# Gate and value of a fused scan and MLP kernel from 15 slice products over three features, instead of 11 over two

## The chip, the cores and the metric

The kernel runs on one core of one Trainium2 chip. The metric is the device time of one execution in microseconds (us): 826.79 us, the median of three runs (826.69 to 827.34). Engines are named as the profile names them: PE (TensorE, matmuls), PEld (its weight loads), DVE (VectorE), ACT (ScalarE), POOL (GpSimd), SP (SyncE, which issues nearly all DMAs). SBUF is the on-chip memory, PSUM the accumulators that PE writes.

## The reference, cut to what matters

Three stages follow one another: a recurrent attention, a first MLP (the largest of three matmuls, then a projection), and a second, gated MLP. All data are fp32, 3072 tokens of width 384; the second MLP has 1536 hidden columns.

```python
def _moe_ref(x, w1, w2, w3, w_out):
    h = np.maximum(np.maximum(x @ w1, x @ w2), x @ w3)
    return (h @ w_out).astype(np.float32)

def _moe2_ref(x, w_gate, w_val, w_out):
    g = x @ w_gate
    silu = g * (1.0 / (1.0 + np.exp(-g)))
    val = x @ w_val
    return (silu * val @ w_out).astype(np.float32)
```

## The kernel before, in words

Tokens are cut into 6 chunks of 512. The first half of the program (to about 400 us) runs attention and the first MLP chunk by chunk and leaves the first MLP's output in DRAM (`y1d`: three K slices of 128 rows for each chunk). The second half is the gated MLP, and it is what the change is about.

Every fp32 factor is split in a high and a low part (`F32R`), and one product of two 128-wide slices is three matmuls of 128x512: high*high, high*low, low*high. The high part is a copy on ACT, the low part a subtraction on DVE or POOL (`op_low`, L795, for the tokens' operands `yo`; `w_low`, L844, for weights; `prod_low`, L924, for the gated product).

A hidden "feature" here is a block of 128 of the 1536 columns, so there are 12. The second half takes two features with two chunks of tokens as one unit: 6 pairs of features by 3 pairs of chunks, 18 units. Gate and value of such a unit would be 2 x 2 x 3 = 12 slice products each (features x chunks x K slices). The kernel does them with 11, by a Strassen-like scheme: sums and differences of weight slices (`w_sum`, on POOL) and of token slices (`y_sum`, on POOL) are multiplied, and the outputs are put together from them. A running sum in PSUM (`px`) is copied out by ACT between its products (`snap`, L894), copies are added on POOL (`mix`, L899), and the other sums (`py`) are added to them by DVE (`join`, L903). Then follow silu on ACT, gate times value on DVE (`times`, L917), the split of the product, and the projection: `proj` makes six outputs (2 chunks x 3 blocks of columns) of 2 x 3 matmuls, which DVE adds up in SBUF (`collect`, L945).

In the first pass over the 12 features (the first pair of chunks) the split weights are made on ACT, DVE and POOL and stored in DRAM; the two later passes load them. Where a pass begins with a new pair of chunks, the operands `yo` are made anew: a POOL sum, a copy on ACT and a subtraction each. Its tile is that of the pass before, so it can be written only when the last product that reads the old one is done.

The order of everything is worked out before the kernel is built. `Plan` holds each step with its engine, an assumed cost, what it depends on and a due time, and `Plan.order` fills one list for each engine by these. It knows when an engine is free, and it treats engines as independent of each other. On the chip every engine runs its list in order: an instruction that waits holds up all that stands behind it. PE's order of products and projections is written out by hand (`SEQ`, `FIRST`, `FINAL`).

Of the kernel before, what the change touches and what calls it, by code (L numbers as in the profile page):

```python
# [29 lines left out]
NQ = 6  # L30
WPARTS = (("a", 6), ("b", 4), ("s", 8), ("p", 6))
# [245 lines left out]
def fused(ctx: ExitStack, tc: tile.TileContext, pk, ub, wt_all, out):  # L277
# [8 lines left out]
    wfd = [dram.tile([128, 2, WCH], F32, name=f"wfd{q}") for q in range(NQ)]  # L286
    wsd = [{s: dram.tile([128, 2, n, C], F32, name=f"wsd{q}{s}") for s, n in WPARTS} for q in range(NQ)]

# [361 lines left out]
    def wload(i):  # L650
        raws[i] = lp.tile([128, WCH, 2], I32, tag="raw", name="raw", bufs=2)
        nc.sync.dma_start(raws[i].rearrange("p n w -> p (n w)"), wt_all[i].bitcast(I32))
# [20 lines left out]
    def words_store(i):  # L673
        q = i - 8
        nc.sync.dma_start(wfd[q // 2][:, q % 2, :].bitcast(I32), fp32s[i])
# [125 lines left out]
    def w_tile(n, s):
        k = dict(WPARTS)[s]
        W[n, s] = rp2[0].tile([128, 2, k, C], F32R, tag=f"u{s}", name=f"W{s}", bufs=2)

    def w_src(n, s):

        w = ws_[n].rearrange("p i (t c) -> p i t c", c=C)
        if s == "a":
            return w[:, 0, 0:6, :]
        if s == "b":  # L810
            return w[:, 1, 0:6, :].rearrange("p (v k) c -> p v k c", v=2)[:, :, 1:3, :]
        if s == "p":
            return w[:, :, 6:9, :]
        return st[n, s]

    def w_dst(n, s, k):
        if s in ("s0", "s1"):
            v = int(s[1])
            return W[n, "s"][:, k, 4 * v:4 * v + 4, :]
        t = W[n, s][:, k]  # L820
        if s == "b":
            return t.rearrange("p (v k) c -> p v k c", v=2)
        return t.rearrange("p (i k) c -> p i k c", i=2) if s == "p" else t

    def w_sum(n, v):

        w = ws_[n].rearrange("p i (t c) -> p i t c", c=C)
        a11, a12, a21, a22 = (w[:, i, 3 * v + k, :] for i in range(2) for k in range(2))
        if n or v:
            st[n, f"s{v}"] = rp2[0].tile([128, 4, C], F32, tag="st", name="st")  # L830
        t = st[n, f"s{v}"]
        g = nc.gpsimd
        g.tensor_tensor(t[:, 0, :], a21, a22, ALU.add)
        g.tensor_tensor(t[:, 1, :], t[:, 0, :], a11, ALU.subtract)
        g.tensor_tensor(t[:, 2, :], a11, a21, ALU.subtract)
        g.tensor_tensor(t[:, 3, :], a12, t[:, 1, :], ALU.subtract)

    def w_high(n, s):
        if s != "s1" and n > 1:
            w_tile(n, s[0])  # L840
        nc.scalar.activation(w_dst(n, s, 0), w_src(n, s), AF.Copy)

    def w_low(n, s, eng):
        eng.tensor_tensor(w_dst(n, s, 1), w_src(n, s), w_dst(n, s, 0).bitcast(F32), ALU.subtract)  # L844

    def w_store(n, s):
        nc.sync.dma_start(wsd[n][s], W[n, s].bitcast(F32))

    def w_load(n, s):
        w_tile(n, s)  # L850
        nc.sync.dma_start(W[n, s].bitcast(F32), wsd[n % NQ][s])

    def mmw(ps, n, s, i, o, first, last):
        d = n // NQ
# [651 lines left out]
```

## Time and profile before

| | us |
|---|---|
| median of three runs | 826.79 (826.69 to 827.34) |
| the profiled execution, its own time | 825.16 |
| its span in the profile | 823.2 |
| PE busy | 804.8 (98%) |
| DVE busy | 580.9 (71%) |
| ACT busy | 429.9 (52%) |
| POOL busy | 230.6 (28%) |

A profile has one row for each instruction. A busy time counts the rows' lengths where they don't overlap. Matmuls overlap: a row of a 128x512 matmul is 0.39 us long, but the next one starts earlier, so what a matmul takes of PE is read from the starts. Releasers (what ended a wait) are worked out from semaphores. The page's own chain of waits is empty in this profile, so the bound is read from the waits of each engine.

### The profile page before, as it was taken

The page shows a single profiled execution, that of the slowest core. Times are in us where ns is not written, and L with a number is a line of the kernel's source. Part 1 is how long each engine was busy: PE and PEld are TensorE (multiplying, and loading weights), DVE is VectorE, ACT ScalarE, POOL GpSimd, SP SyncE. Part 2 cuts the span into 40 slices and gives each one's busy share as a digit, 9 for nine tenths or more (in the row PEclk, how much of TensorE's full clock was granted, in tenths as well). Part 3 has the DMA queues.
Part 4 walks back from the last instruction along what each step waited for, and adds up shares of the span by engine and source line. Part 5 has one row for each costly group of instructions (what it writes and reads, how often), then busy time and mean ns, then how long its engine had stood idle before and what let it go on. Part 6 is the DMA issues. An engine that isn't in the chain of part 4 may idle for free.

```text
span 823.2 us, 15660 instructions
## 1 busy us (share of the span) xinstructions
PE 804.8 (98%) x6248; PEld 659.6 (80%) x6248; DVE 580.9 (71%) x846; ACT 429.9 (52%) x911; POOL 230.6 (28%) x236
## 2 busy tenths in 40 slices
PE   6899999999999999999999999999999999999996
PEld 5687668888888888888888888888888888888885
DVE  7989999987979965458266676773555596455555
ACT  5643464564555643244475544557556785533340
POOL 1000344221132100235565443352122231222120
PEclk9599999999999999999999999999999999999999
DMA  9757474884576543568524444586565555323312
GB/s 289 213 155 230 116 172 138 217 267 101 171 226 165 169 137 116 176 219 320 227 115 151 165 179 179 180 305 261 210 269 225 194 193 191 129 104 128 154 39 80
DMA packets 37807, 149.70 MB, mean 182 GB/s; under 512 B 5312, under 2 KB 8768, under 8 KB 31200
## 3 DMA queue, kind: packets, MB, share of 16 engines
q1 hardware_dynamic: 37584, 148.51, 53.6%
q8 instruction: 51, 0.84, 0.4%
q14 instruction: 28, 0.23, 0.1%
q10 hardware_dynamic: 144, 0.13, 0.0%
HBM read 111.26 MB, written 35.39 MB: 178 GB/s over the span
## 4 chain that ended last, share of the span: by engine, by line


## 5 line engine op out<-in xcount | busy, mean ns | idle before, releaser
L617 PE MATMUL ps<-xh,hi 128*128 128x512 f32 x324 | 130.0, 401 | 0.4 <-DMA xh<-xsh 0.4
L618 PE MATMUL ps<-xl,hi 128*128 128x512 f32 x324 | 127.1, 392 | 0.0
L619 PE MATMUL ps<-xh,lo 128*128 128x512 f32 x324 | 127.0, 392 | 0.0
L858 PE MATMUL px<-yo,Ws 128*128 128x512 f32 x324 | 91.0, 389 | 0.0
L858 PE MATMUL py<-yo,Wa 128*128 128x512 f32 x324 | 85.2, 389 | 0.0
L899 POOL TENSOR_TENSOR sv<-sv 128x512 f32<-128x512 f32 x36 | 48.7, 1353 | 130.4 <-ACT sv L894 118.6
L617 PE MATMUL po<-pr,Wp 128*128 128x512 f32 x216 | 84.1, 390 | 0.2 <-DVE acc L945 0.2
L619 PE MATMUL po<-pr,Wp 128*128 128x512 f32 x216 | 84.0, 389 | 0.0
L618 PE MATMUL po<-pr,Wp 128*128 128x512 f32 x216 | 84.0, 389 | 0.0
L903 DVE TENSOR_TENSOR sv<-py,sv 128x512 f32<-128x512 f32 x54 | 37.2, 689 | 61.9 <-POOL sv L899 42.8
L894 ACT ACTIVATE sg<-px 128x512 f32<-128x512 f32 x72 | 43.1, 598 | 70.6 <-PE px L858 69.6
L945 DVE TENSOR_TENSOR acc<-po,acc 128x512 f32<-128x512 f32 x89 | 60.9, 687 | 26.4 <-PE po L619 26.1
L894 ACT ACTIVATE sv<-px 128x512 f32<-128x512 f32 x72 | 43.0, 598 | 69.9 <-PE px L858 67.1
L899 POOL TENSOR_TENSOR sg<-sg 128x512 f32<-128x512 f32 x36 | 47.2, 1310 | 106.7 <-ACT sg L894 99.0
L924 DVE TENSOR_TENSOR pr<-sg,pr 128x512 fp32r<-128x512 f32 x72 | 54.9, 765 | 30.2 <-ACT pr L921 30.2
L617 PEld LDWEIGHTS ps<-xh,hi 128*128 128x128 f32 x324 | 61.4, 189 | 13.8 <-DMA xh<-xsh 1.1
L619 PEld LDWEIGHTS ps<-xh,lo 128*128 128x128 f32 x324 | 61.3, 189 | 13.0
L903 DVE TENSOR_TENSOR sg<-py,sg 128x512 f32<-128x512 f32 x54 | 37.2, 690 | 48.3 <-POOL sg L899 36.4
L618 PEld LDWEIGHTS ps<-xl,hi 128*128 128x128 f32 x324 | 61.4, 190 | 12.1 <-issue 0.2
L858 PEld LDWEIGHTS px<-yo,Ws 128*128 128x128 f32 x324 | 60.7, 188 | 12.8
L858 PEld LDWEIGHTS py<-yo,Wa 128*128 128x128 f32 x324 | 60.7, 188 | 12.6
L721 DVE TENSOR_TENSOR hw<-hw,ps 128x512 f32<-128x512 f32 x60 | 40.8, 680 | 36.5 <-PE ps L619 28.5
(160 smaller groups left out, 1655.6 us busy)
## 6 DMA issues: line engine op xcount, KB each, us to landing
raw<-wt SPq DMA_DIRECT2D x27, 1152.0 KB, 6.6
inpA<-pk SPq DMA_DIRECT2D x42, 294.0 KB, 5.3
wfd<-fp32s SPq DMA_DIRECT2D x12, 576.0 KB, 4.0
ww<-wfd SPq DMA_DIRECT2D x6, 1152.0 KB, 6.9
inpT<-pk SPq DMA_DIRECT2D x16, 384.0 KB, 4.2
inpV<-pk SPq DMA_DIRECT2D x24, 200.0 KB, 4.1
y1d<-y1s SPq DMA_DIRECT2D x18, 256.0 KB, 4.1
y<-y1d SPq DMA_DIRECT2D x18, 256.0 KB, 4.4
```

Source lines behind the costliest of these rows:

```text
L617: nc.tensor.matmul(ps, lh, rh, start=first, stop=False)
L618: nc.tensor.matmul(ps, lh, rl, start=False, stop=False)
L619: nc.tensor.matmul(ps, ll, rh, start=False, stop=last)
L721: nc.vector.tensor_tensor(hws[f], hws[f], pss[c, f, m], ALU.max)
L858: nc.tensor.matmul(ps, w, x, start=first and k == 0, stop=last and k == 2, skip_group_check=True)
L894: nc.scalar.activation(sbuf(n, v, k), X[n, v], AF.Copy)
L899: nc.gpsimd.tensor_tensor(b, b, buf[n, v, (2, 3)[k]], (ALU.subtract, ALU.add)[k])
L903: nc.vector.tensor_tensor(b, Ys[n, v, k], b, ALU.add)
L924: nc.vector.tensor_tensor(prod[n, k][:, 1, :], gated(n, k), prod[n, k][:, 0, :].bitcast(F32), ALU.subtract)
L945: nc.vector.tensor_tensor(acc[a], t, acc[a], ALU.add)
```

## The change

A unit now has three features and two chunks, and there are 12 units (4 triples of features by 3 pairs of chunks; `NQ` from 6 to 4). Gate and value would be 3 x 2 x 3 = 18 slice products each; a bilinear scheme of rank 15 makes them from 15. The rows of the scheme stand in tables: `ORD` (the order of the 15 products), `CHAIN` (which of six PSUM sums each is added to), `XSUM` (11 sums of token slices, `y_sum`), `WSUM` (9 sums of weight slices for each unit, with 15 additions), `STEPS` (what follows each product: `s` a copy out by ACT, `j` a join by DVE). Three mixes follow for each of gate and value. There are 15 operands `yo` for each pair of chunks in place of 9; `SLOW` says which low parts go to POOL. The projection has three features now: six outputs of 3 x 3 matmuls. The second half's tiles are laid out anew, weights are stored and loaded in parts of five slices (and the projection's apart), and PE's order is given by `seq` and `LASTGAPS`. The first half's rows are the same on every engine until the second half's preparations begin.

```diff
-NQ = 6
-WPARTS = (("a", 6), ("b", 4), ("s", 8), ("p", 6))
+NQ = 4
+NPART = 5
...
+    ORD = (6, 14, 9, 11, 5, 13, 12, 4, 2, 10, 8, 0, 1, 3, 7)
+    CHAIN = "ABDFABDEABCABEC"
...
+    XSUM = ((6, (0, 1), (2, 1), 1), (14, (1, 0), (0, 0), -1), (9, (1, 1), (2, 0), 1), (3, (2, 1), (2, 0), -1),
...
+    WSUM = {9: ((1, 1), (2, 2, 1)), 5: ((1, 0), (0, 2, -1)), 13: ((0, 1), (2, 0, 1)),
...
+    def y_sum(d, r, one_, two, sign):
+        ys2[d, r] = lptile([128, NT], F32, XTAG[r], "xr")
+        nc.gpsimd.tensor_tensor(ys2[d, r], ys2[d, one_], ys2[d, two], ALU.add if sign > 0 else ALU.subtract)
...
+    def op_low(d, i, eng):
+        r = ORD[i]
+        eng.tensor_tensor(op[d, r][:, 1, :], ys2[d, XRAW.get(r, r)], op[d, r][:, 0, :].bitcast(F32), ALU.subtract)
...
+        (f, k), *more = WSUM[r]
+        src = w[:, f, :, k, :]
+        for f, k, sign in more:
+            nc.gpsimd.tensor_tensor(t, src, w[:, f, :, k, :], ALU.add if sign > 0 else ALU.subtract)
+            src = t
...
+    def w_low(n, v, k, eng):
+        for src, h, l in w_pieces(n, v, k):
+            eng.tensor_tensor(l, src, h.bitcast(F32), ALU.subtract)
...
+    def product(n, v, i):
+        r, ch = ORD[i], CHAIN[i]
+        first = ch not in CHAIN[:i]
...
+        for k, (w, x) in enumerate(((lh, rh), (lh, rl), (ll, rh))):
-            nc.tensor.matmul(ps, w, x, start=first and k == 0, stop=last and k == 2, skip_group_check=True)
...
+            nc.tensor.matmul(X[n, v, ch], w, x, start=first and k == 0, stop=k == 2, skip_group_check=True)
...
+    def join(n, v, k, ch, sign):
+        b = buf[n, v, k]
+        if sign > 0:
+            nc.vector.tensor_tensor(b, X[n, v, ch], b, ALU.add)
...
+    def mix(n, v, k):
+        if k == 5:
+            b = sbuf(n, v, 5)
+            (nc.gpsimd if n else nc.vector).tensor_tensor(b, buf[n, v, "d"], buf[n, v, "u"], ALU.subtract)
+        else:
+            b = buf[n, v, k]
+            nc.gpsimd.tensor_tensor(b, b, buf[n, v, "u" if k == 3 else "d"], ALU.add)
...
+    def proj(n, c, m):
+        t = po[n, c, m] = psO[0].tile([128, NT], F32, tag="po", name="po", bufs=2)
+        for e, f in enumerate(((1, 0, 2), (2, 0, 1))[c]):
...
-    UNIT_T = 23.2
+    UNIT_T = 32.66
...
+                slow = n > 0 and v == 1 and k > 0
+                l = L["wl", n, v, k] = on("POOL" if slow else "DVE", 1.75 if slow else 0.85, w_low, n, v, k, nc.gpsimd if slow else nc.vector)(
...
+    SLOW = (4, 6, 8, 10, 12, 14)
...
+        gaps = {(0, 10): 0, (0, 13): 1, (1, 2): 2, (1, 6): 3, (1, 9): 4, (1, 12): 5}
...
+                war = [("x", NQ * d - 1, 1, i)]
...
+        slow = k in ((5, 2, 0) if n == NU - 1 else () if n % NQ == NQ - 1 else (5,))
```

The first place is DVE's list where the second pair of chunks takes over from the first. Before, from the projection sums ahead of the new operands on (`yo` is a new operand's low part, `T`/`y1` its source, `pr` and `sg` the old unit's gated product, `po`/`py` read PSUM):

```order
L945 TENSOR_TENSOR acc_5290<-po_6053,acc_5290 128x512
L795 TENSOR_TENSOR yo_6051<-y1_4730,yo_6051 128x512
L795 TENSOR_TENSOR yo_6062<-y1_4992,yo_6062 128x512
L924 TENSOR_TENSOR pr_6079<-sg_5956,pr_6079 128x512
L945 TENSOR_TENSOR acc_5307<-po_6069,acc_5307 128x512
L795 TENSOR_TENSOR yo_6084<-T2_5006,yo_6084 128x512
L903 TENSOR_TENSOR sv_6099<-py_6092,sv_6099 128x512
L945 TENSOR_TENSOR acc_5331<-po_6106,acc_5331 128x512
L795 TENSOR_TENSOR yo_6113<-y1_4823,yo_6113 128x512
L917 TENSOR_TENSOR sg_6012<-sg_6012,sv_6099 128x512
L795 TENSOR_TENSOR yo_6119<-T4_5095,yo_6119 128x512
```

After, the same place up to the low part of the operand of product 9 (`yo_6332`); `xr` are sums of token slices, `Wp<-wq` low parts of the projection's weights, `L959` is `times` and `L975` `prod_low`:

```order
L959 TENSOR_TENSOR sb_6047<-sb_6047,sb_6224 128x512
L815 TENSOR_TENSOR yo_6257<-xr_6230,yo_6257 128x512
L995 TENSOR_TENSOR acc_5698<-po_6247,acc_5698 128x512
L943 TENSOR_TENSOR sb_6168<-sb_6168,py_6232 128x512
L959 TENSOR_TENSOR sb_6039<-sb_6039,sb_6208 128x512
L815 TENSOR_TENSOR yo_6210<-y1_6019,yo_6210 128x512
L907 TENSOR_TENSOR Wp_6288<-wq_5948,Wp_6288 128x384 x3
L975 TENSOR_TENSOR pr_6277<-sb_6047,pr_6277 128x512
L975 TENSOR_TENSOR pr_6325<-sb_6039,pr_6325 128x512
L959 TENSOR_TENSOR sb_5976<-sb_5976,sb_6115 128x512
L959 TENSOR_TENSOR sb_6014<-sb_6014,sb_6162 128x512
L815 TENSOR_TENSOR yo_6332<-xr_6280,yo_6332 128x512
```

From the second `L959` on, ten instructions without a PSUM operand stand in a row (`Wp` counts three), where before no more than two did here.

The second place is POOL's list beside it. Before (`L899` are mixes, `L788` sums of token slices, `L795` low parts):

```order
L899 TENSOR_TENSOR sv_6076<-sv_6076,sv_6099 128x512
L795 TENSOR_TENSOR yo_6102<-y1_4840,yo_6102 128x512
L899 TENSOR_TENSOR sv_6076<-sv_6076,sv_6129 128x512
L788 TENSOR_TENSOR T1_6177<-y1_6132,y1_6082 128x512
L795 TENSOR_TENSOR yo_6202<-y1_4897,yo_6202 128x512
L899 TENSOR_TENSOR sg_6200<-sg_6200,sg_6231 128x512
```

After (`L806` sums of token slices, `L948`/`L951` mixes, `L815` low parts); `xr_6280` is the sum that `yo_6332` of the first place splits:

```order
L806 TENSOR_TENSOR xr_6230<-y1_6009,xr_6155 128x512
L806 TENSOR_TENSOR xr_6241<-y1_6009,xr_6203 128x512
L815 TENSOR_TENSOR yo_6228<-xr_6203,yo_6228 128x512
L951 TENSOR_TENSOR sb_6168<-sb_6168,sb_6185 128x512
L806 TENSOR_TENSOR xr_6280<-y1_5863,xr_6230 128x512
L806 TENSOR_TENSOR xr_6298<-y1_6016,y1_6019 128x512
L815 TENSOR_TENSOR yo_6187<-y1_5913,yo_6187 128x512
L815 TENSOR_TENSOR yo_6264<-xr_6241,yo_6264 128x512
L815 TENSOR_TENSOR yo_6268<-y1_5863,yo_6268 128x512
L815 TENSOR_TENSOR yo_6342<-xr_6298,yo_6342 128x512
L951 TENSOR_TENSOR sb_6353<-sb_6353,sb_6359 128x512
```

The late sums of token slices stand next to each other now, among four of the six low parts that POOL makes.

The third place is POOL's list in a unit of the first pass. Before, with mixes, one set of weight sums (`L833` to `L836`, 128 columns each, two sets for each unit) and the weights' low parts `Ws`:

```order
L899 TENSOR_TENSOR sg_5184<-sg_5184,sg_5243 128x512
L844 TENSOR_TENSOR Ws_5189<-st_5222,Ws_5189 128x512
L833 TENSOR_TENSOR st_5278<-ww_4971 128x128
L834 TENSOR_TENSOR st_5278<-st_5278,ww_4971 128x128
L835 TENSOR_TENSOR st_5278<-ww_4971 128x128
L836 TENSOR_TENSOR st_5278<-ww_4971,st_5278 128x128
L899 TENSOR_TENSOR sv_5299<-sv_5299,sv_5317 128x512
L899 TENSOR_TENSOR sv_5299<-sv_5299,sv_5340 128x512
L844 TENSOR_TENSOR Ws_5404<-st_5278,Ws_5404 128x512
```

After, the five low parts of weights that POOL makes in such a unit (`L890`), a low part of the gated product, mixes, and the first two of the next unit's 15 additions of weight slices (`L863`):

```order
L890 TENSOR_TENSOR W_5554<-ww_5350,W_5554 128x256
L890 TENSOR_TENSOR W_5554<-st_5435,W_5554 128x256
L890 TENSOR_TENSOR W_5554<-st_5504,W_5554 128x128
L890 TENSOR_TENSOR W_5595<-ww_5350,W_5595 128x128
L890 TENSOR_TENSOR W_5595<-st_5461,W_5595 128x512
L975 TENSOR_TENSOR pr_5608<-sb_5382,pr_5608 128x512
L951 TENSOR_TENSOR sb_5673<-sb_5673,sb_5650 128x512
L948 TENSOR_TENSOR sb_5704<-sb_5691,sb_5650 128x512
L951 TENSOR_TENSOR sb_5679<-sb_5679,sb_5691 128x512
L863 TENSOR_TENSOR st_5727<-ww_5639 128x256
L863 TENSOR_TENSOR st_5736<-ww_5639 128x256
```

Two low parts of 512 columns became five of 128 to 512, and 8 sums of 128 columns became 15 of 256.

## Rows read from the trace of the kernel before

**Rows 1.** The page: engines' busy times, and PE's share and clock in 40 slices.

```profile
PE 804.8 (98%) x6248; PEld 659.6 (80%) x6248; DVE 580.9 (71%) x846; ACT 429.9 (52%) x911; POOL 230.6 (28%) x236
PE   6899999999999999999999999999999999999996
PEclk9599999999999999999999999999999999999999
```

**Rows 2.** Waits of PE from 400 us on: what waited, releaser, us, times, longest.

```profile
PE po L617 <- DVE acc L945: 0.2, 1, 0.2
```

**Rows 3.** Windows, gate and value products alone: stretch, length, PE, PEld, clock, DMA share, GB/s.

```profile
399.80:823.20 423.40, 285.82 (x1188) 222.64 (x1188) 1.00 0.45 170
```

**Rows 4.** Timeline of PE, first and last matmuls of the second half: start us, length us.

```profile
399.89 0.84 PE L858 MATMUL px<-yo,Wa 128*128 128x512 f32 x3
...
816.50 0.39 PE L618 MATMUL po<-pr,Wp 128*128 128x512 f32 x1
816.73 0.39 PE L619 MATMUL po<-pr,Wp 128*128 128x512 f32 x1
```

**Rows 5.** Timeline, DVE and POOL, 550 to 554 us.

```profile
550.17 1.29 POOL L788 TENSOR_TENSOR y<-y,y 128x512 f32<-128x512 f32 x1
...
550.32 1.69 DVE L917 TENSOR_TENSOR sg<-sg,sv 128x512 f32<-128x512 f32 x1
...
551.42 1.75 POOL L899 TENSOR_TENSOR sv<-sv 128x512 f32<-128x512 f32 x1
...
552.71 1.00 DVE L924 TENSOR_TENSOR pr<-sg,pr 128x512 fp32r<-128x512 f32 x1 [0.70 <-ACT pr L921]
...
553.12 1.74 POOL L788 TENSOR_TENSOR T<-y,T 128x512 f32<-128x512 f32 x1
...
553.64 0.68 DVE L903 TENSOR_TENSOR sv<-py,sv 128x512 f32<-128x512 f32 x1
...
554.24 0.67 DVE L945 TENSOR_TENSOR acc<-po,acc 128x512 f32<-128x512 f32 x1
```

**Rows 6.** By line: instructions with their shortest, median and longest duration in ns.

```profile
L917 DVE TENSOR_TENSOR sg<-sg,sv x54: 675/691/1792, 409.7 to 805.4; 128x512 f32<-128x512 f32 x54
L917 DVE TENSOR_TENSOR sg<-sg,px x18: 672/687/689, 419.0 to 806.0; 128x512 f32<-128x512 f32 x18
...
L924 DVE TENSOR_TENSOR pr<-sg,pr x72: 676/691/1779, 411.4 to 808.4; 128x512 fp32r<-128x512 f32 x72
...
L945 DVE TENSOR_TENSOR acc<-po,acc x89: 668/686/692, 443.6 to 815.8; 128x512 f32<-128x512 f32 x89
...
L899 POOL TENSOR_TENSOR sg<-sg x36: 1285/1292/1703, 405.9 to 792.9; 128x512 f32<-128x512 f32 x36
```

**Rows 7.** Windows of one old unit each, first and second pass: PE, PEld, DVE, ACT, POOL.

```profile
446.40:469.60 23.20, 23.20 (x104) 19.22 (x103) 15.62 (x24) 12.47 (x22) 12.13 (x16) 1.00 0.53 192
620.00:643.20 23.20, 23.20 (x104) 19.21 (x103) 13.18 (x21) 14.35 (x27) 5.19 (x4) 1.00 0.54 204
```

**Rows 8.** By line: prices of POOL and DVE for 128 to 768 columns.

```profile
L834 POOL TENSOR_TENSOR st<-st,ww x12: 453/464/968, 356.0 to 493.6; 128x128 f32<-128x128 f32 x12
...
L844 DVE TENSOR_TENSOR Wa<-ww,Wa x6: 957/1020/1214, 359.4 to 490.5; 128x768 fp32r<-128x768 f32 x6
L844 DVE TENSOR_TENSOR Wb<-ww,Wb x6: 682/796/948, 362.0 to 492.5; 128x512 fp32r<-128x512 f32 x6
...
L648 DVE TENSOR_TENSOR lo<-raw,hi x3: 545/552/552, 30.0 to 38.6; 128x384 fp32r<-128x384 f32 x3
```

**Rows 9.** Windows in the first half, columns as in rows 7 (PEclk after POOL).

```profile
28.00:31.40 3.40, 2.70 (x73) 2.23 (x65) 3.32 (x8) 2.37 (x6) 0.00 (x0) 0.50 0.97 366
41.60:45.10 3.50, 3.50 (x21) 3.01 (x20) 2.58 (x5) 1.07 (x5) 0.00 (x0) 1.00 0.75 248
```

**Rows 10.** Timeline of PE, the first dense matmuls of the first half.

```profile
38.52 0.63 PE L618 MATMUL ps<-xl,hi 128*128 128x512 f32 x1
...
41.39 0.39 PE L619 MATMUL ps<-xh,lo 128*128 128x512 f32 x1
```

More of the change, by code (lines that the diff above doesn't have):

```diff
@@ L825, in w_sum @@
[L825 to L836, printed above, removed]
@@ new lines, in unit_words, with p_steps @@
+        return out_
+    def p_steps(n, ld):
+        due = SECOND + UNIT_T * (n + 1) + 3
+        h = on("ACT", 1.3, p_high, n)([ld, close], due, slack=1.0)
+        if n:
+            waits.append((h, [("pj", n - 1, 0, 2), ("wsd", n - 1, "p")]))
+        l = on("DVE", 1.4, p_low, n)([h], due, slack=1.0)
+        L["W", n, "p"] = [l]
+        L["wsd", n, "p"] = dma(128 * 9216, 1, p_store, n)([l], due + 10, slack=3.0)
+        return [h, l]
+    turns_ = []
+    def raw_turn(k):
+        tag = raw_tag(k)
+        old = [j for j in range(k) if raw_tag(j) == tag]
+        return users[old[-1]] if old else []
@@ L1039, in fused @@
     L["bits", 0, 1] = L["bits0", 2, 2]
-    chunks = list(range(1, 8)) + steady + [("unit", q) for q in range(NQ)]
+    chunks = list(range(1, 8)) + steady + [("unit", q) for q in range(NQ)] + [("p", NQ - 1)]
     chunks += [("again", i) for i in range(8)] + [("late", n) for n in range(8)]
@@ L1073, in fused @@
             t0 = START[1] + 20 + STEADY * (i - 8)
-            ld = dma(1152e3, 1, wload, i)(raw_turn(turn), t0, after=t0 - 6)
+            ld = dma(1152e3, 1, wload, i, raw_tag(turn))(raw_turn(turn), t0, after=t0 - 6)
             b = ld
@@ L1346, in finish @@
-    def finish(n, k, deps, due):
-        t = L["times", n, k] = on("DVE", 0.62, times, n, k)(deps + [L["silu", n, k]], due, slack=0.5)
-        war = [("pj", n - 2, k // 2, 2)] if n > 1 else [L["down", 5, 2, 1]] if k or n else [L["up", 5, 4, 2]]
-        if n == 1 and k == 3:
-            war = [L["wfd", 19]]
-        h = on("ACT", 0.53, prod_high, n, k)([t], due + 1, slack=0.6)
-        waits.append((h, war))
-        L["pl", n, k] = on("DVE", 0.62, prod_low, n, k)([h], due + 2, slack=0.5)
-        return t
@@ L1370, in project, with finish @@
-    def project(n, i, due):
-        c, m = divmod(i, 3)
-        deps = [L["pl", n, 2 * c + k] for k in range(2)] + wready(n, "p")
-        turn = 6 * n + i
+    act = {}
+    def finish(n, k, j, due):
+        by = AT_P[n, 0 if k % 2 else 3]
+        if k in (2, 5) and n < NU - 1:
+            by = min(by, AT_X[n + 1, 0, 6])
+        t = L["times", n, k] = on("DVE", 0.74, times, n, k)([j, L["silu", n, k]], by - 3, slack=0.5)
+        if n == NU - 1:
+            war = [("x", n, 1, FINALS.index(k))]
+        elif n:
+            war = [("pj", n - 1, k % 2, 2)]
+        else:
+            war = [L["down", 5, 2, 1]] + (users[18] if k in (1, 3) else [])
+        h = on("ACT", 0.62, prod_high, n, k)([t], by - 2, slack=0.6)
+        waits.append((h, war))
+        slow = k in ((5, 2, 0) if n == NU - 1 else () if n % NQ == NQ - 1 else (5,))
+        L["pl", n, k] = on("POOL" if slow else "DVE", 1.35 if slow else 0.76, prod_low, n, k, nc.gpsimd if slow else nc.vector)([h], by - 1, slack=0.5)
```

607 lines of the change are left out of this document (340 added, 267 removed), and 3 rows, old and new, of the table WSUM.

## The prediction, made before the changed kernel was run

> **What bounds the kernel now.** I read the page first, then PE's waits, then windows and timelines of the second half, which the change is about. PE is busy 98% of the span, at the full clock in all slices but the second [rows 1]. From 400 us on PE waits once, for 0.2 us [rows 2]. So the second half is PE's, and its length is the number of matmuls times the distance of their starts. It has 1188 matmuls of gate and value [rows 3]; the projection adds 18 units x 6 outputs x 6 = 648. The first starts at 399.89, the last at 816.73: 416.8 us for 1835 steps, 0.2272 us each [rows 4]. The 0.39 us that a row shows is not the price: the next matmul starts 0.23 later [rows 4].
>
> The second thing to see lies beside PE. Where a DVE instruction takes both inputs from SBUF, it and POOL's instructions don't run together. At 550.32 a DVE row of 1.69 us begins, and POOL's row that was running ends at 551.46; 0.55 us later DVE's ends. POOL's next row, begun at 551.42, ends 1.16 after DVE's, and so on in turn [rows 5]. Alone the two last 0.68 and 1.29 [rows 6]. So a turn of one POOL and one such DVE instruction takes 1.16 + 0.55 = 1.70 us, while a DVE list that isn't held up starts one every 0.60, as the last two of the rows do [rows 5]. DVE instructions that read PSUM are not held: 89 of them never took over 692 ns, 18 of the same line as the lengthened ones never over 689, against 1792 for that line with both inputs in SBUF [rows 6]. I call the held kind SBUF-only.
>
> The Trainium skill, "SBUF — State Buffer", section "Who interferes with whom", says the same in kind: a VectorE instruction with two SBUF inputs and a GpSimd instruction that reads SBUF share a port, and the second fully blocks until the first is done. This case's trace agrees in kind and gives 1.70 for a pair, not the 1.97 of full lengths; the sum below goes by 1.70, and 1.97 is priced among the rivals.
>
> **The change part by part.** *Removed: matmuls.* New: 12 units x 2 x 15 products x 3 = 1080, old 1188. The projection stays at 12 x 6 x 9 = 648. 108 x 0.2272 = 24.5 us less, if PE stays fed. There is no wait of PE to win beyond that [rows 2], so nothing can come out below that end.
>
> A new unit is 90 + 54 = 144 matmuls, 32.7 us of PE; a product is 0.68 us and an output of the projection 2.04.
>
> *Added beside PE, first pass.* The weights of units 1 to 3 are made beside units 0 to 2. POOL's price for 256 columns isn't in the trace: 128 columns take 0.455 [rows 8] and 512 take 1.29 [rows 6], the line between gives 0.73. I take the line, since DVE's 384, 512 and 768 columns (0.55, 0.68, 0.955) lie on one [rows 8]. For one such unit POOL has 15 additions x 0.73 = 11.0, five low parts of weights 0.73 + 0.73 + 0.455 + 0.455 + 1.29 = 3.7, six mixes 7.7, one low part of the product 1.3: 23.6 us. DVE's SBUF-only work: six `times` and five low parts x 0.68 = 7.5, low parts of weights 4.2 (256 columns 0.405, 128 columns 0.27, both on that line), the projection's weights 3 x 0.55 = 1.65: 13.3 us. Together 36.9 us that exclude each other, for 32.7 us of PE: 4.2 over. Turns give some back: 0.27 for each pair, and if all 25 such DVE instructions came in turn, 30.2 would be left, 92% of the unit. So 0 to 4.2 for each unit. The old unit, reckoned alike, has four mixes, eight sums of 0.455, two low parts (11.4) and on DVE 7 x 0.68 + 2 x 0.955 + 0.68 = 7.4: 18.8 of 23.2 us, 81%, and PE never waited. The trace's own unit has POOL at 12.13 and DVE at 15.62 of 23.2 [rows 7]. A list run in order fills 81% without harm; at 92 to 113% I take it that it can't, all the more as 16 joins and 6 sums of the projection (22 x 0.60 = 13.2 us) stand in the same DVE list, and PE's next product on that sum waits for each join. I take 4 a unit, 12 us for three. With the ends of the price of 256 columns, 0.455 makes this about 0 and 1.29 some 12 a unit; both are far from the line.
>
> *Added, the two turns to a new pair of chunks.* An operand's tile is free when the old unit's product of the same number is done. From the end of value product 0 of the old unit to the turn of product 9 of the new one PE has 23 products and 4 outputs: 23 x 0.68 + 4 x 2.04 = 23.8 us. POOL's late sums can't start at once. The first needs operand 0 written, whose low part stands in DVE's list behind the sum of the third projection output: 2 products and an output (3.4), 0.2 for PE's end to show, 0.60 and 0.68: 4.9 us. That leaves 18.9. In them POOL has 15 instructions (six sums of slices, five low parts, four mixes; the last ten are in the list shown), and DVE 15 SBUF-only ones, the last the low part that product 9 reads, ten of them in a row. 15 x 1.70 = 25.5, less 0.4 since the three `Wp` are 384 columns wide: 25.1, or 6.2 late. Then DVE's list has four more SBUF-only ones up to the operand of product 13, against four of POOL: 6.8 us, where PE has 4 products and an output, 4.8: 2.0 late, and 0.6 for the join between. 8.8 us for the first turn. At the second turn the weights are loaded and the three `Wp` fall away: 15 x 1.16 + 12 x 0.55 = 24.0, 5.1 late, with the rest 7.7 us. 16.5 together. If POOL waited nowhere and DVE's list went at 0.60, both would be 0: POOL's own 15 x 1.29 = 19.4 just fits. Before, the same place had 9 operands and two of the low parts on POOL, and no wait [rows 2].
>
> *PE's clock.* The trace has the lower level only in the first half: in a stretch where PE was idle a fifth of the time it stood at 0.50 (1.2 GHz) [rows 9], and when dense matmuls came, eight ran 0.43 apart (38.52 to 41.08 are six steps) before rows of 0.39 came back [rows 10]. Eight at 0.43 in place of 0.227 cost 1.6 us. The second half had no gap that could bring it down. With stalls of 4 to 6 us it can fall; I take three falls, 4.8 us, between 0 and some 12.
>
> *At nothing.* ACT: 14 copies out, 6 silu, 6 splits a unit at about 0.53 (14.35 us for 27 [rows 7]) are 14 of 32.7 us, and some 8 more for high parts in the first pass. DMA: a unit loads 5.1 MB in 32.7 us, was 3.1 in 23.2, beside a busy share of 0.54 [rows 7]; if late, a stall of some us each. Unit 0's preparation lies beside the first MLP, 0 to 3 us, I take 0. The end has the same forms as before. The units of passes two and three that follow a turn load their weights: POOL 9.0 and DVE 7.5 of 32.7, 50%, no stall.
>
> *Sum.* -24.5 + 12 + 16.5 + 4.8 - 0.2 (the old wait) = +8.6, of which I keep 8.2, since PE's slower matmuls after a stall lie in part beside lists that are late anyway. The profiled execution took 825.16 (span 823.2 and 2.0 around it), so 833.4; the median of the runs stands 1.6 above it: 835.
>
> **The rivals.** *PE stays fed.* The place is the same DVE list, the price a pair; from 18.9 / 15 = 1.26 us a pair downwards the turn fits and the first pass too. Then only the 24.5 count: 802.3. For it speaks that PE never waited before; against it that 1.70 stands in the rows again and again. 0.09.
>
> *Only the turns cost.* The weights of the first pass may be made so far ahead that a late list catches up; then -24.5 + 16.5 + 3.2 - 0.2: 822. For it: the words lie in DRAM early; against: seven weight tiles for six in use leave little room ahead. 0.12.
>
> *The clock stays low.* If it falls at each of some six stalls and PE, slowed, makes later ones, 8 us more: 843. For: the lower level was held in the first half over many short gaps [rows 9]; against: matmuls here are dense. 0.16.
>
> *The pair costs full lengths.* 1.97 in place of 1.70 is 0.27 x 15 x 2 = 8 us more at the turns: 843. This is the page's rule above taken strictly; rows 5 speak against it. 0.03.
>
> *The waits are spread thinner and the two sides cancel*, 826 to 828: 0.04.
>
> The forecast itself: 0.56, 828.5 to 842 by the ends of first pass and clock.
>
> **How the numbers follow.** 835 is the likeliest. From 820 to 846 holds the forecast, the cancelled case, the clock's and strict rule's, and half of the turns-only case: 0.56 + 0.04 + 0.14 + 0.03 + 0.06, a little over 0.8. No change means within 0.2%, 1.65 us, about what this measurement can tell. Faster: 0.09 + 0.11 = 0.20. Within: 0.04. Slower: 0.76.
>
> **What would show it.** Right: 1080 matmuls of gate and value 0.227 apart where PE runs; waits of PE on DVE's joins between 410 and 510 of about 12 us, on operands' low parts (`yo`) at 540 to 555 and again some 140 us later, about 8 each, and hardly any between; SBUF-only rows of DVE near 1.79 and POOL's near 1.7 in these stretches, PSUM-reading ones still under 0.70; the clock at 0.50 behind the longest waits. Wrong: PE without waits over 1 us (802), PE waiting on DMA, or the waits outside these stretches.

## The result, and the profile after

The changed kernel takes 836.2 us, median of four runs (833.7 to 837.0), against 826.75 for the kernel before in four runs of the same comparison: ratio 1.0107, 95% interval 1.0085 to 1.0129. It is slower by 9.45 us, 1.1%. The profiled execution took 836.19, span 834.3. Where the text below gives other times of the kernel before (826.6 to 827.1), they are from the runs beside each experiment.

The page of the changed kernel, against [rows 1]: PE is busy 13 us less, and its share falls from 98% to 95%; POOL's busy time grows by 95 us, DVE's by 78.

```profile
PE 791.7 (95%) x6140; PEld 643.1 (77%) x6140; DVE 659.3 (79%) x931; ACT 459.7 (55%) x997; POOL 325.4 (39%) x294
PE   6799999999999999999979899969999979999997
PEclk9699999999999999999998999989999999999999
```

PE's waits from 395 us on (who waits, releaser, us, times, longest), which answer to [rows 2], first to 515 us, then from there. `yo` L815 is the low part of an operand, `sb` L941 a join:

```profile
PE px L927 <- DVE sb L941: 8.6, 4, 4.3
...
PE px L927 <- DVE yo L815: 11.4, 2, 6.6
PE px L927 <- DVE sb L941: 1.0, 2, 0.7
PE py L927 <- DVE yo L815: 0.5, 1, 0.5
PE py L927 <- POOL yo L815: 0.2, 1, 0.2
```

Before, PE waited 0.2 us here. Now it waits 21.7 us in these rows; all but 0.2 us of that is on DVE, none on a DMA. The windows view of the products alone, and the first and last rows of the second half on PE's timeline, answer to [rows 3, 4]:

```profile
402.00:832.00 430.00, 264.70 (x1080) 0.97 0.54 194
```

```profile
402.07 1.30 PE L927 MATMUL px<-yo,tu 128*128 128x512 f32 x5
...
827.99 0.39 PE L621 MATMUL po<-pr,Wp 128*128 128x512 f32 x1
```

The 108 matmuls are gone (1080 for 1188). From the first product to the last matmul there are 425.9 us, before 416.8: 9.1 more. 1727 steps of 0.2272 would be 392.4, so 33.5 us are not full-speed steps. On PE's timeline I summed by how much each distance of two starts is over 0.2272, where that is 0.3 us or more: 9.65 us before 515 us (the first pass), 8.08 at the first turn (515 to 600), 7.03 at the second (640 to 700), nothing elsewhere. That is 24.8, called waits below; it is more than the 21.7 above, which count only the time in which no matmul's row runs. The other 8.7 are smaller excesses, called slow steps; 6.9 of them lie in the 37 steps made while the clock stood at 0.50. The same sums for all kernels, each from one profiled execution:

| kernel | median of runs, us | first product to last matmul | waits in first pass | first turn | second turn |
|---|---|---|---|---|---|
| before | 826.75 | 416.8 | 0 | 0 | 0 |
| changed | 836.2 | 425.9 | 9.65 | 8.08 | 7.03 |
| e1 mixes on DVE | 825.6 | 414.3 | 4.84 | 7.02 | 3.89 |
| e2 no weight sums | 831.9 | 422.9 | 9.35 | 8.23 | 7.23 |
| e3 waits filled | 838.75 | 427.4 | 9.64 | 4.18 | 5.22 |
| e4 no token sums | 834.1 | 423.2 | 8.5 | 2.9 (and 7.8 for a load) | 2.95 |
| e5 mixes of the first pass on DVE | 827.3 | 415.0 | 4.63 | 5.25 | 7.39 |
| e6 weights' low parts on DVE | 842.25 | 428.9 | 12.97 | 7.72 | 6.90 |
| e7 one input | 832.4 | 421.9 | 10.5 | 5.88 | 4.86 |
| e9 order only | 828.2 | 418.3 | 7.51 | 6.29 | 5.93 |
| e10 places only | 826.0 | 412.8 | 5.96 | 6.72 | 3.87 |
| e8 relieved | 814.05 | 402.2 | 2.01 | 4.09 | 2.04 |

The third column is the one to compare: what the first half takes differs from profile to profile (the first product starts between 399.2 and 404.0 us in these, at 402.1 in the changed kernel's).

At the first turn, timeline of DVE, then of POOL, answering to [rows 5] (start, length, what; a row of x2 or x3 is that many in one line):

```profile
537.93 1.78 DVE L815 TENSOR_TENSOR yo<-y,yo 128x512 fp32r<-128x512 f32 x1
539.64 4.73 DVE L907 TENSOR_TENSOR Wp<-wq,Wp 128x384 fp32r<-128x384 f32 x3
544.29 2.34 DVE L975 TENSOR_TENSOR pr<-sb,pr 128x512 fp32r<-128x512 f32 x2
546.56 1.28 DVE L959 TENSOR_TENSOR sb<-sb 128x512 f32<-128x512 f32 x2
547.77 0.68 DVE L815 TENSOR_TENSOR yo<-xr,yo 128x512 fp32r<-128x512 f32 x1
...
537.41 1.76 POOL L815 TENSOR_TENSOR yo<-y,yo 128x512 fp32r<-128x512 f32 x1
539.12 1.75 POOL L815 TENSOR_TENSOR yo<-xr,yo 128x512 fp32r<-128x512 f32 x1
540.83 1.59 POOL L815 TENSOR_TENSOR yo<-y,yo 128x512 fp32r<-128x512 f32 x1
542.38 1.58 POOL L815 TENSOR_TENSOR yo<-xr,yo 128x512 fp32r<-128x512 f32 x1
543.92 1.57 POOL L951 TENSOR_TENSOR sb<-sb 128x512 f32<-128x512 f32 x1
```

The two engines go in turn: POOL starts one every 1.71 us, 1.55 beside the narrower `Wp`, and DVE with it. Behind the last POOL row, at 545.5, DVE's list goes 0.60 a row once the instruction then held up (the first of the two `pr`) is through. The last DVE row shown is the operand that product 9 reads; PE has waited for it 6.62 us:

```profile
540.60 1.28 PE L927 MATMUL px<-yo,W 128*128 128x512 f32 x4
548.50 1.22 PE L927 MATMUL px<-yo,W 128*128 128x512 f32 x2 [6.62 <-DVE yo L815]
549.52 1.48 PE L927 MATMUL py<-yo,W 128*128 128x512 f32 x3
```

By line (shortest, median, longest in ns), against [rows 6]: `times`, with both inputs in SBUF, is stretched up to 1784; a join, which reads PSUM, never over 692; and the additions of 256 columns on POOL, for which [rows 8] had no row, stand at 0.742.

```profile
L959 DVE TENSOR_TENSOR sb<-sb x71: 675/685/1784, 424.8 to 817.0; 128x512 f32<-128x512 f32 x71
L941 DVE TENSOR_TENSOR sb<-px,sb x95: 673/691/692, 408.8 to 808.7; 128x512 f32<-128x512 f32 x95
L863 POOL TENSOR_TENSOR st<-ww x34: 727/742/1862, 370.1 to 486.4; 128x256 f32<-128x256 f32 x34
```

Row by row, from 400 us on: of 155 DVE rows of 128x512 with both inputs in SBUF, 52 last over 0.8 us, and every one of the 52 overlaps a POOL row; 71 overlap none, and none of the 71 lasts over 0.694. Of 245 rows that read PSUM, 134 overlap a POOL row, and none lasts over 0.693. Before, 17 of 144 lasted over 0.8.

Windows of one unit's length, two in the first pass and one later (PE, PEld, DVE, ACT, POOL, clock), against [rows 7]:

```profile
434.70:467.40 32.70, 29.25 (x116) 23.64 (x117) 23.75 (x34) 20.00 (x44) 22.97 (x25) 0.90 0.21 86
467.40:500.10 32.70, 30.28 (x126) 24.52 (x126) 30.53 (x43) 18.34 (x41) 27.56 (x27) 0.95 0.72 261
582.00:614.70 32.70, 32.70 (x146) 27.05 (x146) 17.95 (x28) 23.58 (x42) 9.14 (x7) 1.00 0.66 240
```

A busy time here has in it what an instruction was held up, so these don't tell how much room is left. I therefore also took the time in which POOL or a DVE instruction with both inputs in SBUF runs, overlaps counted once, over three units' length (98.1 us) from the first product on. It is 88.3 us, 90%.

The clock, in windows behind the longest waits, against [rows 9]. It stood at 0.50 (1.2 GHz) in four stretches of the second half, each of them at or behind one of the four longest waits; before, there was no such stretch:

```profile
435.80:442.60 6.80, 5.38 (x13) 0.50 0.14 55
...
476.80:480.20 3.40, 3.40 (x10) 0.50 1.02 429
545.10:551.90 6.80, 3.40 (x8) 0.50 0.59 214
685.00:691.80 6.80, 4.03 (x10) 0.50 0.23 74
```

What the first pass waits for is seen at the longest of its waits. PE, POOL and DVE, 431 to 438 us:

```profile
431.44 1.77 DVE L975 TENSOR_TENSOR tq<-sb,tq 128x512 fp32r<-128x512 f32 x1
433.13 3.43 DVE L959 TENSOR_TENSOR sb<-sb 128x512 f32<-128x512 f32 x2
436.48 1.28 DVE L941 TENSOR_TENSOR sb<-px,sb 128x512 f32<-128x512 f32 x2
...
431.05 1.60 POOL L951 TENSOR_TENSOR sb<-sb 128x512 f32<-128x512 f32 x1 [2.70 <-DVE sb L943]
432.62 1.71 POOL L948 TENSOR_TENSOR sb<-sb 128x512 f32<-128x512 f32 x1
434.30 1.71 POOL L951 TENSOR_TENSOR sb<-sb 128x512 f32<-128x512 f32 x1
...
437.22 1.22 PE L927 MATMUL px<-yo,W 128*128 128x512 f32 x2 [4.31 <-DVE sb L941]
```

POOL had been idle for 2.70 us; then its three mixes of the new half unit come, and meet three instructions of the old unit in DVE's list (a low part, two `times`). Each of these takes 1.7 in place of 0.60, and the join that PE needs stands behind them. That is a meeting of two short lists, not a full unit.

The second longest wait, 2.42 us at 476.4, has the same make: three mixes, and two `times` that last 3.45 together. At 459.4 (0.94 us) two mixes hold up low parts of weights ahead of the join. The last of the four, 0.97 us at 512.6, is of another kind: there the join itself waited for a mix on POOL.

```profile
511.82 0.69 DVE L941 TENSOR_TENSOR sb<-px,sb 128x512 f32<-128x512 f32 x1 [1.03 <-POOL sb L948]
```

### The profile page after: what moved, and what is told of

It is laid out like the page before. It is cut to its first block, busy times and chain, and to the rows that moved or that the text cites. A ratio compares the mean times of both kernels' runs of the same rounds, so it can differ in the third digit from the quotient of the medians.

```text
span 834.3 us, 15790 instructions
## 1 busy us (share of the span) xinstructions
PE 791.7 (95%) x6140; PEld 643.1 (77%) x6140; DVE 659.3 (79%) x931; ACT 459.7 (55%) x997; POOL 325.4 (39%) x294
## 4 chain that ended last, share of the span: by engine, by line
PE 80%; DVE 12%; issue 2%; POOL 2%; ACT 1%; DMA 1%; SPq 0%; DVEq 0%; POOLq 0%; ACTq 0%
PE px L927 12%; PE ps L619 11%; PE py L927 10%; PE ps L620 10%; PE ps L621 10%; PE po L619 5%; PE po L621 5%; PE po L620 5%; DVE sb L959 2%; PE ps L740 2%; PE y L509 2%; PE kp L483 2%; DVE yo L815 2%; PE sc L565 1%; PE sc L469 1%
## 5 line engine op out<-in xcount | busy, mean ns | idle before, releaser
L927 PE MATMUL px<-yo,W 128*128 128x512 f32 x519 | 137.2, 399 | 21.2 <-DVE yo L815 11.4
L927 PEld LDWEIGHTS px<-yo,W 128*128 128x128 f32 x519 | 98.2, 191 | 45.7 <-DVE sb L941 12.8
L951 POOL TENSOR_TENSOR sb<-sb 128x512 f32<-128x512 f32 x46 | 69.1, 1505 | 148.4 <-ACT sb L936 95.3
L927 PE MATMUL py<-yo,W 128*128 128x512 f32 x456 | 125.9, 396 | 0.7 <-DVE yo L815 0.5
L927 PEld LDWEIGHTS py<-yo,W 128*128 128x128 f32 x456 | 87.1, 191 | 20.0 <-DVE yo L815 0.9
L941 DVE TENSOR_TENSOR sb<-px,sb 128x512 f32<-128x512 f32 x95 | 63.7, 685 | 21.7 <-PE px L927 18.7
L936 ACT ACTIVATE sb<-px 128x512 f32<-128x512 f32 x96 | 56.3, 597 | 35.0 <-PE px L927 31.5
L972 ACT ACTIVATE pr<-sb 128x512 fp32r<-128x512 f32 x70 | 42.8, 634 | 43.5 <-DVE sb L959 43.4
L959 DVE TENSOR_TENSOR sb<-sb 128x512 f32<-128x512 f32 x71 | 63.6, 919 | 0.3
L955 ACT ACTIVATE sb<-sb 128x512 f32<-128x512 f32 x72 | 44.4, 630 | 29.7 <-DVE sb L941 29.3
```

What stands on the lines that cost most here:

```text
L927: nc.tensor.matmul(X[n, v, ch], w, x, start=first and k == 0, stop=k == 2, skip_group_check=True)
L936: nc.scalar.activation(sbuf(n, v, k), X[n, v, ch], AF.Copy)
L941: nc.vector.tensor_tensor(b, X[n, v, ch], b, ALU.add)
L951: nc.gpsimd.tensor_tensor(b, b, buf[n, v, "u" if k == 3 else "d"], ALU.add)
L955: nc.scalar.activation(b, b, AF.Silu)
L959: nc.vector.tensor_tensor(g, g, buf[n, 1, k], ALU.mult)
```

## The experiments

All are made from the changed kernel. They ask two things: whether the exclusion of POOL and DVE (POOL and a DVE instruction with both inputs in SBUF don't run together) makes the waits, and whether it does so by the load as a whole or by what stands ahead of a join. Where a step changes its engine, its price or its date, the planner draws up all lists anew, so such an edit changes the order of other steps too. In e3 and e7 the order of DVE's and POOL's lists stays; in e2 too, but for the steps that make weights.

**e1, mixes on DVE.** In effect:

```diff
-            nc.gpsimd.tensor_tensor(b, b, buf[n, v, "u" if k == 3 else "d"], ALU.add)
+            nc.vector.tensor_tensor(b, b, buf[n, v, "u" if k == 3 else "d"], ALU.add)
-            L["mix", n, v, 3] = on("POOL", 1.35, mix, n, v, 3)(...)
+            L["mix", n, v, 3] = on("DVE", 0.75, mix, n, v, 3)(...)
```

(and the mixes 4 and 5 alike)

> The 70 mixes that POOL does (0.68 us on DVE, 1.5 on POOL in the run of the changed kernel, 1.29 undisturbed) go to DVE; nothing is left out. Theory (the waits come from POOL and DVE instructions with both inputs in SBUF excluding each other): POOL loses six instructions a unit, DVE gains six short ones, the turns of a pair get fewer and no join waits for a lengthened mix any more; time about 823 (818 to 828), waits of PE on joins before 515 us from 9.7 to under 5 us, POOL's busy time from 325 to about 220. Rival (DVE's list is simply too long, POOL has no part in it): DVE gets 6 x 0.68 = 4.1 us more a unit where it is late already, three units and two turns, so 845 or more.

Measured: 825.6 us, ratio to the kernel before 0.9988 (0.9969 to 1.0007), 10.6 below the changed kernel. POOL's busy time fell to 226.6. DVE, the engine that PE waits for, was given 70 more instructions, and PE waits less: 15.8 us in place of 24.8. That DVE's list is simply too long is therefore not the cause. With it goes the lengthening: 35 of its 225 rows with both inputs in SBUF last over 0.8 us, against 52 of 155. That the exclusion is the cause goes with both, but e1 alone doesn't part it from the new order of the lists, which e9 shows to be worth several us by itself.

**e2, no weight sums.** Units 1 to 3 take raw slices where sums stood; the steps that read the sums are pointed at raw slices too.

```diff
         for f, k, sign in more:
+            if n == 0:
-            nc.gpsimd.tensor_tensor(t, src, w[:, f, :, k, :], ...)
+                nc.gpsimd.tensor_tensor(t, src, w[:, f, :, k, :], ...)
```

> The 15 additions of weights on POOL are left out for units 1 to 3 (the weights then come from raw slices). Theory of the prediction (the first pass is late because 36.9 us of work that excludes itself stand against 32.7 of PE): 11.0 us a unit go, 25.9 are left, 79%, and PE's waits before 515 us (9.6 us) vanish, with one or two falls of the clock: 822 to 826. Rival (what is late in the first pass is the path of a mix: PE waits for a join, the join for a mix on POOL that stands behind another mix, each lengthened by DVE's list): the sums are not on that path, the waits of about 4.5 us at 432 and 2.6 at 473 stay, 833 to 836.

Measured: 831.9 us, just below the rival's 833 to 836, and the waits of the first pass are as they were, 9.35 for 9.65. The windows of the two kernels from 400 to 414 and 428 to 442 us (PE, PEld, DVE, ACT, POOL), first the changed kernel, then e2:

```profile
400.00:414.00 14.00, 14.00 (x63) 11.38 (x62) 9.45 (x15) 11.80 (x25) 12.55 (x16) 1.00 0.62 246
...
428.00:442.00 14.00, 9.69 (x33) 7.54 (x32) 12.87 (x16) 6.71 (x12) 10.28 (x11) 0.78 0.57 191
```

```profile
400.00:414.00 14.00, 13.94 (x62) 11.23 (x61) 9.49 (x20) 12.97 (x28) 3.17 (x2) 1.00 0.49 193
...
428.00:442.00 14.00, 10.57 (x41) 8.26 (x40) 11.27 (x13) 6.44 (x11) 4.97 (x3) 0.88 0.43 132
```

In these windows POOL is busy a quarter and a half as long, and the same wait stands in the same place (434.26, 3.43 us on a join; the two `times` ahead of it take 3.43 again). The time in which POOL or a DVE instruction with both inputs in SBUF runs falls from 90% to 64% of the three units. The prediction's reason for the first pass, a load of 36.9 us in 32.7, falls here. The 3.1 us by which the second half is shorter are nearly all slow steps: the half-speed stretch behind that wait has 7 steps, not 12, and the second stretch is missing.

**e3, the waits filled.**

```diff
+    FILL = {(4, 0, 8): 22, (8, 0, 8): 16}
+        for k in range(fill):
+            nc.tensor.matmul(X[n, v, ch], lh, rh, start=False, stop=k == fill - 1, ...)
```

> At the two turns, behind product 8 of units 4 and 8, 22 and 16 more matmuls are issued (into the same sum, which they change), 38 x 0.227 = 8.6 us of PE in the place of its waits for product 9's operand. Theory (the late list is not PE's, and the clock falls behind the long waits): the falls to 0.50 near 545 and 685 us go away, the end comes 2 to 5 us earlier, 831 to 834, although PE has more to do. Rival (the clock's fall costs nothing since the lists are late anyway): 836. Rival (the waits are made by PE itself, through joins that follow its products): 840 to 845.

Measured: 838.75 us, 1.5 more in the second half. At the first turn the clock stayed up (windows of e3, columns as in the windows above):

```profile
540.00:554.00 14.00, 10.75 (x45) 7.76 (x44) 14.00 (x14) 4.14 (x8) 10.37 (x7) 1.00 0.76 279
...
694.00:708.00 14.00, 13.29 (x52) 10.55 (x53) 9.90 (x15) 9.05 (x17) 0.88 (x2) 0.88 0.32 93
```

It gained nothing. From PE's timeline of e3:

```profile
548.72 0.73 PE L930 MATMUL px<-yo,W 128*128 128x512 f32 x2 [1.70 <-DVE yo L815]
...
553.91 1.67 PE L930 MATMUL px<-yo,W 128*128 128x512 f32 x6 [1.56 <-DVE sb L946]
555.41 0.39 PE L930 MATMUL py<-yo,W 128*128 128x512 f32 x1
```

Product 9 starts at 548.72, where the changed kernel has it at 548.50, and the next two at 553.91 and 555.41 for 553.68 and 555.18: 0.23 later each time. The first product of e3 is itself 0.39 later (402.46 for 402.07), so counted from there they come 0.16 us earlier, not 2 to 5. What the changed kernel lost to slow matmuls, e3 waits at the join. My theory, 2 to 5 us back, was wrong; at this fall the rival (it costs nothing) is right. The other rival, that PE makes the waits itself, falls with the same rows, although the time lies near its 840: with 22 more matmuls ahead of it, the operand of product 9 came when it had come before. At the second turn the clock's fall only moved, to 695.1 to 698.6 us, behind the turn; that goes with the 1.5 us, but isn't shown to be their cause. The falls of the first pass weren't tried.

**e4, no token sums at the turns** (the planner's price for them goes to 0.01).

```diff
+        if d:
+            ys2[d, r] = ys2[d, one_]
+            return
         ys2[d, r] = lptile([128, NT], F32, XTAG[r], "xr")
```

> At the two turns the 11 sums of slices on POOL are left out (the operands are split from raw slices); POOL's and DVE's low parts stay. Theory (15 pairs of 1.70 against 18.9 us): POOL has 9 instructions where it had 15, the list is in time but for 1 to 3 us a turn; the waits on operands' low parts (11.4 us) go to under 4 and the time to 824 to 828. Rival (DVE's own list of 15 instructions, or the high parts on ACT, or the loads of the slices): the waits stay above 8 us and the time at 834 to 836.

Measured: 834.1 us, and yet the waits on operands went from 11.9 to 2.2 us and the two turns from 15.1 to 5.8. The time was eaten by one new wait of 7.4 us at 567.6. There ACT, whose list was drawn up anew, stood 9.28 us at an instruction (L703, `sign_check`) that reads matrices still to be loaded, and a copy out stood behind it:

```profile
571.20 1.31 ACT L703 ACTIVATE raw<-raw,tiny 128x1152 f32<-128x1152 f32 x1 [9.28 <-DMA raw<-wt]
```

So the turns go as the theory has it, and the time was forecast wrong: the new list of ACT made a wait that the theory didn't have.

**e5, the mixes of units 0 to 3 alone on DVE** (the edit of e1 under `if n < 4`).

> Only the mixes of units 0 to 3 go to DVE; those of units 4 to 11 stay on POOL; nothing is left out. Theory (in the first pass PE waits for a join, and the join stands behind DVE instructions that POOL's mixes of the same half unit lengthen): waits before 515 us from 9.65 to 2 to 4, the first turn about as it was (5 to 8), the second turn untouched at 7.0; time 824 to 827. Rival (the first pass is late by its whole load on POOL and DVE, as the prediction has it): 18 mixes of 22 us less on POOL, 12 us more on DVE, in three units of which each is 4 over: waits before 515 us about halved at best (5 or more), 829 to 834.

Measured: 827.3 us, ratio 1.0001 (0.9986 to 1.0017), just above the theory's 824 to 827. The first pass falls to 4.63, a little above the theory's 2 to 4 and below the rival's 5; the second turn stays at 7.39. The second half is 10.9 us shorter: 5.0 us less in the waits of the first pass, 2.8 at the first turn, whose old unit is unit 3, 3.4 in slow steps, and 0.4 lost at the second turn. Beside e2 it says which work counts: 22 mixes moved (28 us of POOL at 1.29) did what 33 us of sums left out did not. How much of it the new order of the lists did is open.

**e6, weights' low parts on DVE.**

```diff
-                slow = n > 0 and v == 1 and k > 0
+                slow = False
```

> The five low parts of weights a unit that POOL does in the first pass go to DVE: POOL loses 3.7 us a unit, DVE gets 2.0; nothing is left out. Theory (what counts is what stands in DVE's list ahead of a join, and none of the five stands on a path of PE while it is POOL's): PE's waits before 515 us grow from 9.65 to 11 to 15, time 837 to 842. Rival of the prediction (36.9 us of work that excludes itself in 32.7): 1.7 us a unit less, waits shrink by up to 5, time 831 to 834.

Measured: 842.25 us (836.4 to 845.4), the first pass waits 12.97. The profiled run is the lowest of the four, so its trace shows at most part of what the median lost. By the load it should have got better. It got worse, as the order theory said: what had been POOL's now stands in DVE's list ahead of joins. At the longest wait low parts of weights of 256 columns stand there, beside sums and mixes on POOL; two of them take 1.69 us together, where one alone takes 0.41:

```profile
490.26 1.69 DVE L890 TENSOR_TENSOR W<-ww,W 128x256 fp32r<-128x256 f32 x2
...
496.40 1.65 PE L927 MATMUL px<-yo,W 128*128 128x512 f32 x3 [5.30 <-DVE sb L941]
```

**e7, one input.** The low parts of operands that DVE makes at the turns are products with 0.0, so they are zero.

```diff
+        if d and eng is nc.vector:
+            eng.tensor_scalar(op[d, r][:, 1, :], ys2[d, XRAW.get(r, r)], 0.0, None, ALU.mult)
+            return
```

> At the two turns the nine low parts of operands on DVE read one input (a product with 0.0 in place of the difference, so the low parts are zero). Theory (only a DVE instruction with both inputs in SBUF and POOL exclude each other): these nine last under 0.70 beside POOL, POOL's sums beside them about 1.3, and the turns' waits go from 15.1 to 8 to 11; time 828 to 832. Rival (any DVE instruction that reads SBUF is held up): they last up to 1.8 as before, 835 to 837.

Measured: 832.4 us, the turns' waits 10.7. The time is just above where my theory put it, and the theory's reason is wrong. By line, the new form:

```profile
L816 DVE TENSOR_SCALAR yo<-xr x14: 411/862/1524, 523.1 to 690.6; 128x512 fp32r<-128x512 f32 x14
```

It takes 0.41 alone and is held up to 1.52 beside POOL. So one SBUF input doesn't free a DVE instruction. It won time because it is shorter by 0.27, in each turn with POOL too (1.52 for 1.78). DVE's and POOL's lists have the order of the changed kernel here, so the turns' 4.4 us less come from the shorter instructions, not from a new order.

**e8, the relieved kernel.** All mixes on DVE, and:

```diff
-    SLOW = (4, 6, 8, 10, 12, 14)
+    SLOW = (4, 6, 8)
-        slow = k in ((5, 2, 0) if n == NU - 1 else () if n % NQ == NQ - 1 else (5,))
+        slow = k in ((5, 2, 0) if n == NU - 1 else () if n % NQ == NQ - 1 else ())
-        due = SECOND + UNIT_T * n - 14
+        due = SECOND + UNIT_T * n - 18
-  ... y_sum, d, r, one_, two, sign)(deps, base - 12 + MM * ORD.index(r), slack=1.0)
+  ... y_sum, d, r, one_, two, sign)(deps, base - 16 + MM * ORD.index(r), slack=1.0)
```

> All mixes on DVE; at the turns only 3 of the low parts of operands stay on POOL instead of 6, the low part of the product goes to DVE, and the planner gets the weights' preparation due 4 us and the token sums 4 us earlier; nothing is left out. Theory (PE's waits are made by pairs of POOL and two-input DVE instructions, which get few when POOL keeps only sums): waits of PE in the second half from 23 to about 9 us, slow matmuls from 8 to under 3, time 811 to 816, below the kernel before. Rival (DVE, at 23 us more work, becomes the bound): 826 or more.

Measured: 814.05 us (812.2 to 814.9), ratio to the kernel before 0.9846 (0.9822 to 0.9870): faster than both kernels, with nothing left out. Its page and PE's waits:

```profile
PE 788.1 (97%) x6140; PEld 642.4 (79%) x6140; DVE 675.7 (83%) x1019; ACT 457.4 (56%) x997; POOL 202.8 (25%) x206
```

```profile
PE px L927 <- DVE sb L941: 3.7, 6, 1.3
PE px L927 <- ACT sb L936: 1.2, 1, 1.2
PE px L927 <- DVE yo L815: 0.8, 1, 0.8
PE py L927 <- DVE yo L815: 0.5, 2, 0.2
```

The second half takes 402.2 us, 14.7 less than before and 9.8 above its matmuls. Against the changed kernel it has 16.6 us less of waits and 7.1 less of slow steps; its clock stands at 1.00 from the first product to the last matmul.

**e9 and e10, its two ingredients apart:** the two dates alone, and the places alone.

> Of the relieved kernel only the two dates of the planner are kept (weights' preparation 4 us earlier, token sums 4 us earlier); every instruction stays on its engine, so the work and the number of possible pairs are those of the changed kernel. Theory of load (POOL and DVE together have too much at these places, whatever the order): within 2 us of 836. Theory of order (a wait arises where a lengthened DVE instruction happens to stand ahead of a join, so another order of the same work gives other waits): some of the 23 us of waits go, 827 to 832.

> Of the relieved kernel only the places are kept (all mixes on DVE, 3 low parts of operands on POOL in place of 6, low part of the product on DVE); the planner's dates are those of the changed kernel. Theory of load: this alone brings what the relieved kernel has, 812 to 817. Theory of order: the dates are worth about 7 us here too, 819 to 823.

Measured: e9 828.2 us (ratio 1.0008, 0.9993 to 1.0024), e10 826.0 (1.0000, 0.9984 to 1.0017). Against the changed kernel the order alone is worth 8.0 us, with the same work on the same engines; the places alone 10.2; both together 22.1, 3.9 more than the two added. For e9 the theory of order holds. For e10 both were wrong: its median lies above either forecast. Its profile is of the lowest of ten runs (822.4, median 826.0); in it, waits of 3.2 us at 409 and 3.5 from 521 on stand where e8 has 1.3 and 0.8, which is about 4.5 of the 10.6 us between the two second halves.

## Why the prediction was right, and where its reasons were not

The time (835 forecast, 836.2 measured), the sign and the cause in kind (PE waits for DVE's late joins and low parts, which POOL holds up) were right. That the time came within 1.2 us is in part luck. Step by step:

- *Matmuls, -24.5.* Right: 108 fewer, and the same 0.2272 a step where PE runs.
- *The turns, 8.8 and 7.7.* 8.08 and 7.03. Product 9 was to be 6.2 and 5.1 late, its steps were 6.79 and 4.91 too long. The pair at 1.70 is 1.71 in the rows; the full lengths (1.97) would be 0.26 more. The count is right as well, 15 POOL rows and 15 of DVE from 522.5 us to the operand of product 9, but they didn't go as 15 pairs: ten of DVE's fifteen were lengthened, five went at 0.60. POOL was through after 23.0 us, not 25.1. What filled the 26.0 us up to the operand was DVE's own list, with ten PSUM-reading rows between, which the sum had left out (6 us at 0.60). The two misses nearly cancel. e4 and e7 show both sides of the pair: fewer POOL instructions, or shorter ones of DVE, and the turn gets shorter. Small misses: 2.0 up to product 13 was too much, and shorter waits of 0.3 to 0.9 took its place.
- *The first pass, 12.* 9.65 in size, but the step from 36.9 us of work in 32.7 to 4 us of wait a unit failed. The work that excludes itself filled 88.3 of 98.1 us, 29.4 a unit, so it did fit: the step's own lower end (30.2, 0 over) was nearer. And the waits don't follow it: it is 90% of the three units in the changed kernel, 64% in e2, 83% in e6, 94% in e9, 86% in e8, and the waits there are 9.65, 9.35, 12.97, 7.51 and 2.01. What PE waited for, in all but 0.97 us of its four waits, was the join behind DVE instructions that POOL's mixes stretch at that moment; e5, which moves these mixes alone, removed half of it. Of the price of 256 columns the line was right: 0.73 forecast, 0.742.
- *The clock, 4.8.* Four falls, not three, and 8.7 us of slow steps, 6.9 of them at 0.50. But e3 shows that the fall at the first turn cost nothing: PE, slowed, ran beside a list that was late anyway. So slow steps and waits partly stand in for each other: the clock's term was 3.9 too small, the waits' 3.7 too large, and the sum came out. The prediction had allowed for such cover with 0.4 us (8.2 of 8.6 kept). What the falls of the first pass cost by themselves stays open.
- *What held.* The sum by the trace is -24.5 + 24.8 + 8.7 = +9.0 for the second half, forecast -24.5 + 12 + 16.5 + 4.8 - 0.2.
- *At nothing.* ACT, DMA and the end: no wait of PE on a DMA in the second half, as forecast. The first product started 2.2 us later than in the profile of before, which lies within what the other kernels' profiles scatter (399.2 to 404.0); the medians differ by 9.45.
- *The rivals.* PE stays fed (802): no, although e8 comes to 814. Only the turns cost (822): no. The clock stays low (843): it came back each time; the four stretches above have 8 to 13 matmuls.

One word in it was wrong besides. I called the held kind SBUF-only with both inputs from SBUF; e7 shows a DVE instruction with a single SBUF input held as well.

## What to carry to other kernels

Moving a step from POOL to DVE can speed up a kernel whose PE waits for DVE, when the two engines exclude each other (e1), or slow it down (e6): count what of POOL's work meets DVE's list just ahead of an instruction that PE needs, not the busy shares. A planner that treats such engines as independent draws up lists that look free and aren't; with the same work, another order was worth 8 us here. And before a term is written for the clock, look whether the list that PE waits for is later than PE: then slow matmuls are covered.

## What the runs showed of the hardware that I had not expected

- A DVE instruction with one SBUF input of 128x512 fp32 took 0.41 us alone and up to 1.52 beside POOL (e7). The Trainium skill, "SBUF — State Buffer", section "Who interferes with whom", names besides two SBUF inputs a second case in which VectorE holds the shared port, a two-port performance mode. These rows agree with it, though none of them tells the mode.
- The clock's fall behind a wait of 6.6 us at the first turn made eight matmuls slow, and the products behind them no later (e3).
- The second half's first product came between 399.2 and 404.0 us in the profiles of twelve kernels, though no edit was made to the first half's own work; an edit of the second half is better read from its own length than from the whole time.
